# Queries and keys prepared one quad further ahead, sums of squares later, the 1e-6 added on VectorE

## The chip, the cores and the metric

The kernel runs on one core of one Trainium2 chip. The time is the device time of one launch in microseconds (us). Several runs of each kernel are made; the median is compared. One further execution is recorded by the hardware profiler, and the views shown here come from that one.

## The reference, cut to what matters

Cosine attention for 8 batches of 12 heads, 448 tokens, head size 64, followed by a two-layer network with an exact GELU over all 3584 tokens:

```
q_n = q / (norm(q) + 1e-6);  k_n = k / (norm(k) + 1e-6)
attn = softmax(q_n @ k_n.T / 0.1)            # per head, 448 x 448
x = concat of heads of (attn @ v)            # 3584 x 768
h = x @ w_in                                 # 768 -> 2048
out = gelu(h) @ w_out                        # 2048 -> 768
```

All inputs and the output are float32; the matrix products run in bf16.

## The kernel before

**Quads, units, groups.** Four heads of one batch form a *quad*; a batch has three, so there are 24, and batch b begins with quad g0 = 3b. A *unit* is what one preparation step handles: quad 0 is split in two units, and from then on unit n is quad n - 1. In `attention(b)`, `u = 3b + 1` is the unit of quad g0; in `first(b)`, `u` is the unit of the next batch's first quad. Units are put into *groups* of one or two, whose norms go through the logarithm and the exponential together.

**Preparing a quad.** `load_qk` (SyncE queue, L130) brings q and k; `square` squares both on GpSimd (L157, one instruction for 128x1792 elements); `reduce` sums each row's 64 squares on VectorE (L166). For a group, `logs` and `roots` take exp(0.5 ln(.)) on ScalarE (L173, L179 or L182), `inverses` adds 1e-6 and inverts (from group 4 on the addition is a GpSimd instruction, L191; the reciprocal is VectorE's, L193). `scale` multiplies q and k by it on GpSimd (L209, two instructions a quad) and `transposes` turns the result with a transposing DMA from the SyncE queue (L221), which gives `qkT`. Buffers: 4 for loaded quads, 2 for squares, 3 each for scaled and for turned quads.

**Attention.** `scores` (L247) makes four 64x448 products for one chunk of keys into one of three pairs of PSUM banks; `exps` (L257) takes the exponential on ScalarE. `visit(b, pairs)` does this for as many of the 21 chunks of batch b as it has pairs named, in the order of the quads; a pair can be written again when its exponential is done. `total(g)` sums the exponentials with TensorE (`sm`, L309, 16 products) and turns, adds, inverts and spreads them on VectorE (L331 to L352). `weighted(g, p)` multiplies with v (`o`, L323, 28 products) into pair p and normalises into `x` on VectorE (L357). For the first quad of a batch from the fourth batch on, the sums are taken on VectorE instead (`chunked`, L266, two instructions; `turned_all`, `inverted_all`), during `first`.

**The two layers.** `first(b)` multiplies x by w_in (`hp`, L759, 96 products) and applies GELU. The second layer (`op`, L392) is cut into single products and used as filling of the next batch's attention: `run()` issues the next 12 to 28 of them. Sixteen make one tile of 128x384, which VectorE copies out (`ot`, L396) before SyncE stores it. For every second batch the filling has 128 products (8 tiles), for the others 96 (6 tiles); I number the tiles and their copies 1 to 8 within a batch.

**Two PSUM banks are shared.** `mm_tile` gives the `op` tiles two banks in turn, and `sm` takes the bank that the next `op` tile would get:

```
t = ps_mm.tile(list(shape), dtype, tag=f"mm{turn[0] if aside is None else turn[0] ^ aside}", name=name)
if aside is None:
    turn[0] ^= 1
```

So `sm` and the next `op` tile must wait until the copy of the tile before last is done.

**Order.** `tc.manual_schedule()` keeps every engine's instructions in the order in which the program writes them. `upto(f, n)` calls step f for all units, quads or groups below n that are not done yet; where it stands decides where on every queue these instructions come.

Of the kernel before, what the change touches and what calls it, by code (L numbers as in the profile page):

```python
# [9 lines left out]
F32 = mybir.dt.float32  # L10
BF16 = mybir.dt.bfloat16
AF = mybir.ActivationFunctionType
ALU = mybir.AluOpType
# [3 lines left out]
def kernel(  # L17
# [17 lines left out]
    nc = tc.nc  # L35
    B, H, S, D = q.shape
    C = S // D
    NQ = H // 4
# [9 lines left out]
    consts = ctx.enter_context(tc.tile_pool(name="consts", bufs=1))  # L48
# [4 lines left out]
    nrm = ctx.enter_context(tc.tile_pool(name="nrm", bufs=3))  # L53
# [32 lines left out]
    nc.vector.memset(blank, 0.0)  # L86

    root2 = [consts.tile([128, 4 * C, 2], F32, name=f"root2_{n}") for n in range(2)]
    for t in root2:
        nc.vector.memset(t[:, :, 1], 1e-6)  # L90

# [21 lines left out]
    units = [(0, 0, 1), (0, 1, 2)] + [(g, 0, 2) for g in range(1, NG)]  # L113
    NU = len(units)
    groups = [[n] for n in range(NQ + 2)] + [[NQ + 2, NQ + 3], [2 * NQ + 1], [2 * NQ + 2]]
    for n in range(3 * NQ, NU, NQ):
        groups += [[n, n + 1], [n + 2]] if n + 2 < NU else [[n]]
    shapes = [[len(gr), 2, units[gr[0]][2] - units[gr[0]][1], C] for gr in groups]
    place = {u: (n, j) for n, gr in enumerate(groups) for j, u in enumerate(gr)}
    qk_t, v_t, sq_t, nq_t, rn_t, qkb_t, qkT_t, pt_t = {}, {}, {}, {}, {}, {}, {}, {}  # L120
# [47 lines left out]
    ln_t, sr_t = {}, {}  # L168
# [5 lines left out]

    def roots(n):
        ln = ln_t.pop(n)
        if n <= NQ:
            sr_t[n] = root2[n % len(root2)][:, :math.prod(shapes[n])]
            nc.scalar.activation(sr_t[n][:, :, 0], ln.rearrange("p j i s c -> p (j i s c)"), AF.Exp, scale=0.5)  # L179
        else:  # L180
            sr_t[n] = nrm.tile(list(ln.shape), F32, tag="sr", name=f"sr{n}")
            nc.scalar.activation(sr_t[n], ln, AF.Exp, scale=0.5)  # L182

    def inverses(n):
        sr = sr_t.pop(n)
        shape = [128] + shapes[n]
        se = nrm.tile(shape, F32, tag="se", name=f"se{n}")
        if n <= NQ:
            nc.vector.tensor_reduce(se.rearrange("p j i s c -> p (j i s c)"), sr, mybir.AxisListType.X, ALU.add)
        else:  # L190
            nc.gpsimd.tensor_scalar(se, sr, 1e-6, None, ALU.add)  # L191
        rn = nrm.tile(shape, F32, tag="rn", name=f"rn{n}")
        nc.vector.reciprocal(rn, se)  # L193
        rn_t[n] = rn
# [68 lines left out]
    def chunked(g, s):  # L263
        if s == 0:
            acc_t[g] = accp.tile([128, 2, S], F32, tag="acc", name=f"acc{g}")
        nc.vector.tensor_reduce(acc_t[g][:, s], all_t[g][:, :, s].rearrange("p c q -> p q c"),  # L266
                                mybir.AxisListType.X, ALU.add)

    def turned_all(g):
        tr = rcp.tile([128, 2 * NB, 32], F32, tag="tr", name=f"ta{g}")  # L270
        nc.vector.transpose(tr.rearrange("p b r -> p (b r)"), acc_t.pop(g).rearrange("p s q -> p (s q)"))
        su = bank_t[g, "su"] = rcp.tile([128, 2, 2, NB], F32, tag="sa", name=f"sa{g}")
        nc.vector.tensor_reduce(su[:, 0].rearrange("p s b -> p (s b)"), tr, mybir.AxisListType.X, ALU.add)
        for j in range(4):
            o = j ^ 1
            nc.vector.tensor_copy(su[32 * j:32 * (j + 1), 1], su[32 * o:32 * (o + 1), 0])

    def inverted_all(g):
        su = bank_t.pop((g, "su"))
# [49 lines left out]
    def turned(g):  # L329
        tr = rcp.tile([128, 2 * NB, 32], F32, tag="tr", name=f"tr{g}")[:, :NB]  # L330
        nc.vector.transpose(tr.rearrange("p b r -> p (b r)"), bank_t.pop((g, "sm"))[:, :S])  # L331
        bank_t[g, "tr"] = tr.rearrange("p b (k r) -> p k b r", k=2)
# [26 lines left out]
    def total(g):  # L359
        sums(g)  # L360
        turned(g)
        inverted(g)
        spread(g, 0)
        spread(g, 1)
# [75 lines left out]
    def upto(f, n, last=None):  # L440
        last = {load_qk: NG, load_v: NV, root: len(groups), load_wi: NQ + 1, load_wo: 4}.get(f, NU)
        while done.get(f, 0) < min(n, last):
            done[f] = done.get(f, 0) + 1
            f(done[f] - 1)
# [188 lines left out]
    def visit(b, pairs):  # L633
        for p in pairs:
            n, c = passes[at.get(b, 0)]
            at[b] = at.get(b, 0) + 1
            scores(b * NQ + n, ((0, c), (1, c)), p)
            exps(b * NQ + n, ((0, c), (1, c)))

    def attention(b, fill):  # L640
        fill = list(fill)
        if b == 1:
            parts = iter((20, 13, 14, 17, 16, 16))
        elif b == 2:
            parts = iter((20, 16, 16, 16, 16, 14, 14, 16))
        else:
            parts = iter((20, 18, 18, 18, 26, 28) if len(fill) == 128 else (14, 12, 14, 14, 20, 22))

        def run(n=None):
            for _ in range(next(parts) if n is None else n):  # L650
                fill.pop(0)()

        x_t[b] = xp.tile([128, KD, S], BF16, tag="x", name=f"x{b}")
        g0, u = b * NQ, b * NQ + 1
        run()
        upto(scale, u + 3)
        upto(transposes, u + 3)
        if b == 1:
            upto(load_qk, g0 + NQ + 2)
            upto(square, u + 4)  # L660
            visit(b, (0, 1, 2))
            run()
            visit(b, (0, 1, 2))
            run()
            upto(load_qk, g0 + NQ + 3)
            visit(b, (0, 1))
            upto(square, u + 5)
            run()
            visit(b, (0, 1, 2))
            both(g0, 0)  # L670
            upto(load_v, b + 3)
            upto(load_qk, g0 + NQ + 4)
            visit(b, (1, 2))
            upto(reduce, u + 4)
            run()
            visit(b, (1, 2, 0))
            both(g0 + 1, 1)
            visit(b, (2, 0))
            logs(6)
            roots(6)  # L680
            run()
            both(g0 + 2, 2)
            inverses(6)
            done[root] = 7
            return
        upto(scale, u + 4)
        upto(transposes, u + 4)
        if b == 2:
            visit(b, (0, 1, 2))
            run()  # L690
            upto(load_qk, g0 + NQ + 3)
            upto(square, u + 5)
            visit(b, (0, 1, 2))
            run()
            total(g0)
            visit(b, (1, 2))
            weighted(g0, 0)
            upto(load_v, b + 3)
            visit(b, (1, 2))
        else:  # L700
            visit(b, (1, 2))
            weighted(g0, 0)
            visit(b, (1, 2))
            run()
            upto(load_qk, g0 + NQ + 3)
            upto(square, u + 5)
            visit(b, (0, 1, 2))
            upto(load_v, b + 3)
        run()
        visit(b, (0, 1, 2))  # L710
        upto(reduce, u + 5)
        run()
        upto(load_qk, g0 + NQ + 4)
        total(g0 + 1)
        visit(b, (1, 2))
        weighted(g0 + 1, 0)
        visit(b, (1, 2))
        n = 2 * b + 5
        if b == 2:
            run()  # L720
            visit(b, (0,))
            total(g0 + 2)
            visit(b + 1, (1, 2))
        else:
            run()
            if b + 1 < B:
                visit(b + 1, (1, 2, 0))
            total(g0 + 2)
            if b + 1 < B:
                visit(b + 1, (1,))  # L730
        if n < len(groups):
            logs(n)
            roots(n)
            inverses(n)
            done[root] = n + 1
        if b == 2:
            run()
            visit(b + 1, (0, 1, 2))
        run()
        if b + 1 < B:  # L740
            visit(b + 1, (1, 2))
        weighted(g0 + 2, 0)
        if b + 1 < B:
            visit(b + 1, range(1, 1 + C - at[b + 1]))
        assert not fill, len(fill)

    def first(b):
# [4 lines left out]
        u = (b + 1) * NQ + 1  # L752
# [19 lines left out]
        if b == 0:  # L772
            upto(square, u + 3)
            upto(scale, u + 1)
            upto(transposes, u + 1)
            upto(load_wo, 4)
            upto(reduce, u + 3)
        else:
            late = int(b == 1)
            upto(scale, u + 2 - late)  # L780
            upto(transposes, u + 2 - late)
            upto(load_qk, (b + 1) * NQ + 5)
            upto(square, u + 4 - late)
            if 1 < b < B - 1:
                chunked((b + 1) * NQ, 0)
                chunked((b + 1) * NQ, 1)
            upto(reduce, u + 4 - 2 * late)
            if 1 < b < B - 1:
                turned_all((b + 1) * NQ)
                inverted_all((b + 1) * NQ)  # L790
# [34 lines left out]
    late = nrm.tile([128, 1], F32, tag="late", name="late", bufs=1)  # L825
# [56 lines left out]
```

## Time and profile before

| | |
|---|---|
| median of 3 runs | 422.19 us (421.31 to 422.74) |
| profiled execution, its own time | 422.47 us |
| its span from the first to the last instruction | 420.7 us |
| granted TensorE clock, mean | 1.0 |
| busy: TensorE, VectorE, ScalarE, GpSimd | 405.1, 253.0, 248.5, 167.5 us |
| instructions: TensorE, VectorE, ScalarE, GpSimd | 3423, 409, 362, 115 |
| from one batch's first `hp` to the next, batches 2 to 6 | 54.4, 48.4, 50.6, 48.4, 50.6 us |

1.8 us of the profiled time lie outside the span. The last row is read from the timeline of TensorE; the first `hp` of batches 1 to 6 are at 79.59, 133.95, 182.39, 233.00, 281.44 and 332.04 us, and the last batch's is at 376.73 us. The odd batches 3, 5 and 7 have the short filling. A line of the timeline reads: start, duration, engine, line of the program, operation, tiles, shapes, how many instructions are merged, and in brackets how long the engine was idle before and what ended that. The ends of TensorE's products are modelled, so the starts are what is read.

### The profile page before, as it was taken

Reading aid. Unit: us, or ns where it says so; the run is one execution under the profiler, and the core shown is the slowest. Engines: PE = TensorE matmul, PEld = TensorE weight load, DVE = VectorE, ACT = ScalarE, POOL = GpSimd, SP = SyncE. Lnnn points to the kernel's source line nnn. Section 1 sums busy time; section 2 is a strip of 40 time slices with the busy share of each in tenths; the row PEclk is TensorE's granted clock in tenths of the full one; section 3 lists DMA queues with packets and bytes.
Section 4 is the critical chain, followed back from the end, with each engine's and each line's share of the span. In section 5 each row is a group of like instructions: output and inputs, shape, how many; then the busy total and the mean of one; then the engine's idle time right before and its main releaser. Section 6 shows DMA issues by size and latency. Waiting matters only on the chain.

```text
span 420.7 us, 8110 instructions
## 1 busy us (share of the span) xinstructions
PE 405.1 (96%) x3423; PEld 212.0 (50%) x3423; DVE 253.0 (60%) x409; ACT 248.5 (59%) x362; POOL 167.5 (40%) x115
## 2 busy tenths in 40 slices
PE   8999999999999997999999998899999999999995
PEld 3445445555445553555555554455555555455563
DVE  5786117922666993689556894669845795360021
ACT  6995786388667575655674657575665557714300
POOL 5999615193907228080641707244180603000000
PEclk9999999999999999999999999999999999999999
DMA  8999999552693306950197802954069400330032
GB/s 291 260 256 211 202 232 305 122 132 45 122 272 108 110 1 139 263 150 24 30 187 226 170 0 47 244 158 127 2 126 221 89 0 2 83 77 1 6 77 70
DMA packets 66484, 54.53 MB, mean 130 GB/s; under 512 B 38672, under 2 KB 62352, under 8 KB 66448
## 3 DMA queue, kind: packets, MB, share of 16 engines
q1 hardware_dynamic: 54464, 41.79, 37.8%
q0 software_dynamic: 11600, 11.80, 17.4%
q8 instruction: 27, 0.44, 0.4%
q10 hardware_dynamic: 384, 0.43, 0.3%
q14 instruction: 9, 0.07, 0.1%
HBM read 45.61 MB, written 11.01 MB: 135 GB/s over the span
## 4 chain that ended last, share of the span: by engine, by line
PE 52%; issue 18%; POOL 16%; DMA 6%; ACT 5%; DVE 1%; SPq 1%; POOLq 0%; ACTq 0%; DVEq 0%
PE hp L759 22%; PE op L392 20%; POOL qkb L209 8%; POOL sq L157 6%; PE st L247 4%; DMA qkT<-qkb 4%; ACT pt L257 4%; PE o L323 2%; PE sm L309 2%; DMA qk<-in_k_dram 2%; PE op L411 1%; SPq L130 1%; ACT L815 1%; POOL v L142 1%; POOL se L191 1%
## 5 line engine op out<-in xcount | busy, mean ns | idle before, releaser
L257 ACT ACTIVATE pt<-st 128x896 bf16<-128x896 f32 x168 | 142.7, 916 | 63.6 <-PE st L247 63.2
L392 PE MATMUL op<-wo,g 128*128 128x384 bf16 x864 | 148.2, 327 | 0.0
L759 PE MATMUL hp<-x,wi 128*128 128x448 bf16 x768 | 147.1, 353 | 0.0
L392 PEld LDWEIGHTS <-g 128*128 128x128 bf16 x864 | 81.3, 98 | 62.0 <-issue 10.8
L759 PEld LDWEIGHTS <-wi 128*128 128x128 bf16 x768 | 74.4, 98 | 71.7 <-issue 3.3
L802 ACT ACTIVATE g<-hp 128x448 bf16<-128x448 f32 x128 | 65.3, 546 | 75.4 <-PE hp L759 75.1
L209 POOL TENSOR_TENSOR qkb<-qk,rn 128x896 bf16<-128x896 f32 (+1 forms) x50 | 80.2, 1630 | 15.0 <-DVE rn L193 15.0
L396 DVE COPY ot<-op 128x384 f32<-128x384 f32 x54 | 29.2, 544 | 81.6 <-PE op L392 79.5
L157 POOL TENSOR_TENSOR sq<-qk 128x1792 f32<-128x1792 f32 (+1 forms) x22 | 66.5, 3037 | 13.0 <-DMA qk<-in_k_dram 13.0
L191 POOL TENSOR_SCALAR se<-sr 128x28 f32<-128x28 f32 (+1 forms) x15 | 4.5, 302 | 156.8 <-ACT sr L182 156.8
L166 DVE TENSOR_REDUCE nq<-sq 128x28 f32<-128x1792 f32 (+2 forms) x30 | 48.4, 1636 | 22.7 <-POOL sq L157 18.9
L247 PE MATMUL st<-qkT 64*64 64x448 bf16 x672 | 51.9, 360 | 4.9 <-DMA qkT<-qkb 3.2
L266 DVE TENSOR_REDUCE acc<-pt 128x448 f32<-128x3136 bf16 x10 | 55.3, 5572 | 0.0
L323 PE MATMUL o<-pt,v 64*64 64x448 bf16 x672 | 36.8, 350 | 0.0
L357 DVE TENSOR_TENSOR x<-o,rs 128x448 bf16<-128x448 f32 x48 | 27.5, 609 | 12.0 <-PE o L323 11.7
L247 PEld LDWEIGHTS <-qkT 64*64 64x64 bf16 x672 | 17.8, 105 | 32.7 <-issue 21.7
L352 DVE STREAM_TRANSPOSE rs<-rc 128x448 f32<-128x448 f32 x48 | 28.1, 623 | 0.8
L323 PEld LDWEIGHTS <-v 64*64 64x64 bf16 x672 | 19.3, 107 | 12.7 <-issue 1.7
L331 DVE STREAM_TRANSPOSE tr<-sm 128x448 f32<-128x448 f32 x19 | 12.3, 648 | 22.1 <-PE sm L309 19.8
L309 PE MATMUL sm<-pt,ones 128*32 128x448 bf16 (+1 forms) x256 | 13.9, 332 | 3.7 <-DVE ot L396 3.5
L193 DVE RECIPROCAL rn<-se 128x28 f32<-128x28 f32 (+2 forms) x19 | 6.9, 364 | 14.3 <-POOL se L191 13.7
L343 DVE TENSOR_REDUCE tr<-tr 32x28 f32<-32x28 f32 x64 | 12.6, 196 | 1.2
(48 smaller groups left out, 144.0 us busy)
## 6 DMA issues: line engine op xcount, KB each, us to landing
qk<-in_q_dram SPq DMA_DIRECT2D x23, 448.0 KB, 6.4
qk<-in_k_dram SPq DMA_DIRECT2D x23, 448.0 KB, 7.9
out_dram<-ot SPq DMA_DIRECT2D x48, 192.0 KB, 3.4
v<-in_v_dram POOLq DMA_DIRECT2D x7, 672.0 KB, 12.1
wo<-in_moe_w_out_dram POOLq DMA_DIRECT2D x4, 768.0 KB, 13.4
wi<-in_moe_w_in_dram POOLq DMA_DIRECT2D x4, 512.0 KB, 13.8
out_dram<-ot SPq DMA_DIRECT2D x12, 96.0 KB, 2.1
wi<-in_moe_w_in_dram POOLq DMA_DIRECT2D x4, 256.0 KB, 14.1
```

The lines of the kernel that those rows point to most:

```text
L157: eng.tensor_tensor(sq[:, part], t[:, part], t[:, part], ALU.mult)
L166: nc.vector.tensor_reduce(nq[:, part], sq[:, part], mybir.AxisListType.X, ALU.add)
L209: eng.tensor_tensor(qkb[:, i, :, s0:s1].rearrange("p c s d -> p s c d"), t[:, i, s0:s1], rn[:, i].to_broadcast([128, s1 - s0, C, D]), ALU. ...
L247: nc.tensor.matmul(st[cols, n, :S], lhsT=qkT[rows, 1, c, cols], rhs=qkT[rows, 0, :, cols], start=True, stop=True, tile_position=(64 * s, 6 ...
L257: nc.scalar.activation(pt, st[:, :, :S], AF.Exp, scale=inv_tau)
L266: nc.vector.tensor_reduce(acc_t[g][:, s], all_t[g][:, :, s].rearrange("p c q -> p q c"), mybir.AxisListType.X, ALU.add)
L323: nc.tensor.matmul(bank_t[g, h][cols, :S], lhsT=v_t[g][rows, s, c, :], rhs=pt_t[g, s, c][rows], start=(c == 0), stop=(c == C - 1), tile_po ...
L352: nc.vector.transpose(rs, bank_t[g, "rc"][:, h].to_broadcast([128, NB, 32]))
L392: nc.tensor.matmul(ps[:, :NH], lhsT=g_t[sb][:, kf, t * 128:(t + 1) * 128], rhs=wo[:, kf, ni * NH:(ni + 1) * NH], start=(kf == 0), stop=(kf ...
L396: nc.vector.tensor_copy(ot[:, ni * NH:(ni + 1) * NH], ps[:, :NH])
L759: nc.tensor.matmul(hps[m], lhsT=wi[:, kd, m * 128:(m + 1) * 128], rhs=x_t[b][:, kd, :], start=(kd == 0), stop=(kd == KD - 1))
L802: nc.scalar.activation(g_t[sb][:, m, hf * S:(hf + 1) * S], hps.pop(m), AF.Gelu)
```

## The change

- `groups` are cut differently from unit 11 on: the pairs are the second and third quad of a batch, the single one is the first quad of the next batch. Before, the single one was the second quad, the pair the third and the next batch's first.
- In `first(b)`, b from 2 on, two quads are scaled and turned, where one was; at the head of the next `attention` one is left of two. Loads go one quad further ahead.
- The squares go one unit further ahead: `attention(b)` still holds one and `first(b)` two, but unit u + 4's now stands in `first(b - 1)` and unit u + 5's in `attention(b)`, after the load of v (batch 2 holds both). Of the reductions, `attention(b)` now holds two and `first(b)` one: unit u + 4's stands ahead of the third `run()` (the fourth in batch 2), unit u + 5's after `weighted(g0 + 1, 0)` and a `visit`, just ahead of the fifth `run()` (the sixth in batch 2). In `first` the one reduction stands between the two `chunked`.
- `visit(b, (1, 2))` stands ahead of `total(g0 + 1)`, where it stood behind it (in batch 2 also at `total(g0)`).
- From group 4 on the 1e-6 is added by a VectorE reduction over pairs (value, 1e-6), as it was for the earlier groups: the GpSimd instruction is gone. The four copies in `turned_all` become reductions over one element.

```diff
@@ root2
+    root2 += [consts.tile([128, 8 * C, 2], F32, name=f"root4_{n}") for n in range(1)]
@@ groups
-    for n in range(3 * NQ, NU, NQ):
-        groups += [[n, n + 1], [n + 2]] if n + 2 < NU else [[n]]
+    groups += [[3 * NQ, 3 * NQ + 1]]
+    for n in range(3 * NQ + 2, NU, NQ):
+        groups += [[n, n + 1], [n + 2]] if n + 2 < NU else [[n, n + 1]]
@@ roots(n)
-        if n <= NQ:
-            sr_t[n] = root2[n % len(root2)][:, :math.prod(shapes[n])]
-            nc.scalar.activation(sr_t[n][:, :, 0], ln.rearrange("p j i s c -> p (j i s c)"), AF.Exp, scale=0.5)
-        else:
-            sr_t[n] = nrm.tile(list(ln.shape), F32, tag="sr", name=f"sr{n}")
-            nc.scalar.activation(sr_t[n], ln, AF.Exp, scale=0.5)
+        sr_t[n] = root2[2 if len(groups[n]) == 2 else n % 2][:, :math.prod(shapes[n])]
+        nc.scalar.activation(sr_t[n][:, :, 0], ln.rearrange("p j i s c -> p (j i s c)"), AF.Exp, scale=0.5)
@@ inverses(n)
-        if n <= NQ:
-            nc.vector.tensor_reduce(se.rearrange("p j i s c -> p (j i s c)"), sr, mybir.AxisListType.X, ALU.add)
-        else:
-            nc.gpsimd.tensor_scalar(se, sr, 1e-6, None, ALU.add)
+        nc.vector.tensor_reduce(se.rearrange("p j i s c -> p (j i s c)"), sr, mybir.AxisListType.X, ALU.add)
@@ turned_all(g)
-            nc.vector.tensor_copy(su[32 * j:32 * (j + 1), 1], su[32 * o:32 * (o + 1), 0])
+            nc.vector.tensor_reduce(su[32 * j:32 * (j + 1), 1].rearrange("p s b -> p (s b)"),
+                                    su[32 * o:32 * (o + 1), 0].rearrange("p s (b n) -> p (s b) n", n=1),
+                                    mybir.AxisListType.X, ALU.add)
@@ attention(b)
         if b == 2:
             visit(b, (0, 1, 2))
             run()
-            upto(load_qk, g0 + NQ + 3)
+            upto(load_qk, g0 + NQ + 4)
             upto(square, u + 5)
             visit(b, (0, 1, 2))
             run()
+            visit(b, (1, 2))
             total(g0)
-            visit(b, (1, 2))
             weighted(g0, 0)
             upto(load_v, b + 3)
             visit(b, (1, 2))
@@
             run()
-            upto(load_qk, g0 + NQ + 3)
-            upto(square, u + 5)
+            upto(load_qk, g0 + NQ + 4)
             visit(b, (0, 1, 2))
             upto(load_v, b + 3)
+        upto(square, u + 6)
+        upto(reduce, u + 5)
         run()
         visit(b, (0, 1, 2))
-        upto(reduce, u + 5)
         run()
-        upto(load_qk, g0 + NQ + 4)
+        upto(load_qk, g0 + NQ + 5)
+        visit(b, (1, 2))
         total(g0 + 1)
-        visit(b, (1, 2))
         weighted(g0 + 1, 0)
         visit(b, (1, 2))
+        upto(reduce, u + 6)
@@ first(b)
             late = int(b == 1)
-            upto(scale, u + 2 - late)
-            upto(transposes, u + 2 - late)
+            if b == 1:
+                upto(scale, u + 1)
+                upto(transposes, u + 1)
+            for n in range(2, 4) if b > 1 else ():
+                upto(scale, u + n)
+                upto(transposes, u + n)
+                upto(load_qk, (b + 1) * NQ + 6)
             upto(load_qk, (b + 1) * NQ + 5)
-            upto(square, u + 4 - late)
+            upto(square, u + 3 if b == 1 else u + 5)
             if 1 < b < B - 1:
                 chunked((b + 1) * NQ, 0)
+                upto(reduce, u + 4)
                 chunked((b + 1) * NQ, 1)
```

## The prediction

> **What bounds the kernel now.** I read the page first: TensorE is busy 405.1 of 420.7 us, the others 60% or less, so the end moves only with TensorE's stops. The waits, asked for TensorE alone, name them (total, times, longest):
>
> ```profile
> PE sm L309 <- DVE ot L396: 3.5, 2, 1.8
> PE st L247 <- DMA qkT<-qkb: 3.2, 4, 1.1
> ```
>
> The timeline of TensorE places them. In batch 3:
>
> ```profile
> 159.77 2.45 PE L392 MATMUL op<-wo,g 128*128 128x384 bf16 x14
> 163.35 0.76 PE L247 MATMUL st<-qkT 64*64 64x448 bf16 x12 [1.13 <-DMA qkT<-qkb]
> 164.04 2.45 PE L392 MATMUL op<-wo,g 128*128 128x384 bf16 x14
> 168.25 0.85 PE L309 MATMUL sm<-pt,ones 128*32 128x448 bf16 x16 [1.76 <-DVE ot L396]
> 169.03 0.57 PE L247 MATMUL st<-qkT 64*64 64x448 bf16 x8
> 169.43 1.50 PE L323 MATMUL o<-pt,v 64*64 64x448 bf16 x28
> 170.75 0.87 PE L247 MATMUL st<-qkT 64*64 64x448 bf16 x8
> 171.56 3.42 PE L392 MATMUL op<-wo,g 128*128 128x384 bf16 x20
> ```
>
> Starts, not ends, give the prices. Unstopped, 14 `op` take 2.37 to 2.38, 16 `sm` 0.78, 28 `o` 1.33, 12 `st` 0.69, 8 `st` 0.46 (0.40 where `o` follows). So the first stop costs 163.35 - 159.77 - 2.37 = 1.21, the second 168.25 - 164.04 - 2.37 = 1.84, and the 8 `st` at 170.75 take 0.81, 0.35 too long: their pair waits for the exponential of the `st` at 169.03. Batch 5 repeats all three, batch 7 the first (0.86) and third; 4, 6 and, twice, 2 have the third only. VectorE shows who made the second:
>
> ```profile
> 165.71 2.02 DVE L166 TENSOR_REDUCE nq<-sq 128x28 f32<-128x1792 f32 x1 [4.20 <-POOL sq L157]
> 167.65 0.55 DVE L396 COPY ot<-op 128x384 f32<-128x384 f32 x1
> ```
>
> A reduction stood at the head of VectorE's queue waiting for GpSimd's square; the copy behind it frees the bank that `sm` wants. This is the pattern to carry into the changed order.
>
> **The change, batch by batch.** All starts below are the rows of before, moved by what has gone or come earlier.
>
> *Batches 3 and 5, gains.* The second quad is turned during `first`, so qkT is there: -1.21. The reduction ahead of the third `run` has a square finished in `first`: -1.84. `st` ahead of `sm` puts 0.40 + 0.78 + 1.33 between it and the next `st`, against 0.44 to ScalarE's start and two exponentials of 0.87: -0.35. Together -3.40.
>
> *Batches 3 and 5, what is late next.* The second reduction now stands between the normalisation of g0 + 1 and copy 4. In before, `turned` to the end of `weighted` takes VectorE 169.15 to 173.43, 4.28. From the batch's first `op` TensorE needs 2.37 + 0.40 + 1.33 + 0.80 + 2.05 + 0.69 + 2.37 + 0.69 + 2.37 + 0.40 = 13.5 up to `sm` (the first long `st`, at 0.80, stays). `turned` follows 0.90 behind, so `weighted` ends at 13.5 + 0.90 + 4.28 = 18.7; the reduction takes 1.95, to 20.6; copy 4 0.55, to 21.2. `sm` of g0 + 2 wants that bank at 20.0 (13.5 + 0.78 + 1.33 + 0.46, then 20 `op` 3.3 and 12 `st` 0.69): 1.2 of stop. Net -2.2 each.
>
> *Batches 4 and 6.* Gain 0.35. Copy 5 stands behind the same reduction. `sm` comes 3.34 + 0.40 + 1.33 + 0.80 + 3.03 + 0.69 + 3.03 + 0.69 + 3.03 + 0.40 = 16.74 after the first `op`: normalisation ends at 16.74 + 0.90 + 4.28 = 21.9, the reduction at 23.9, copy 5 at 24.45. Tile 7 wants its bank after 16.74 + 0.78 + 1.33 + 0.46 = 19.31 and 22 `op` more, at 22.9. Stop 1.6, net +1.2 each. In before copy 5 ended 1.1 ahead of tile 7, so 1.95 does not fit in.
>
> *Batch 7.* No reduction is left: -0.86 - 0.35 = -1.2.
>
> *Batch 2.* Gain 0.35 twice. But here the second reduction is quad 11's, whose square waits for a load issued in this very batch; the square and the load were followed by an idle stretch before. Rows (SyncE's timeline, the issues with their us to landing, TensorE's timeline):
>
> ```profile
> 114.73 0.61 SPq L130 DMA_DIRECT2D qk<-in_k_dram  x1
> qk<-in_k_dram SPq DMA_DIRECT2D x1, 448.0 KB, 8.4
> 121.76 2.45 PE L392 MATMUL op<-wo,g 128*128 128x384 bf16 x14
> 124.14 0.38 PE L247 MATMUL st<-qkT 64*64 64x448 bf16 x4
> 124.54 0.84 PE L309 MATMUL sm<-pt,ones 128*32 128x448 bf16 x14
> 125.84 0.57 PE L247 MATMUL st<-qkT 64*64 64x448 bf16 x8
> ```
>
> k of quad 11 lands at 114.73 + 8.4 = 123.1; SyncE's queue ahead of it (two turning DMAs, one store) is unchanged. Square 3.17, to 126.3; reduction 2.0, to 128.3; copy 6 0.6, to 128.9; only then `sm`. TensorE is at that `sm` at 123.6 (124.14 + 0.19 for 4 `st`, less 0.7): 5.3 us of standstill. The next `st` start at 128.9 + 0.78 = 129.7 instead of 125.84: +3.85. The reduction ahead of the fourth `run` has its square at 113.8 and ends at 116.6; copy 4 at 117.1 is just in time for tile 6 at 117.3.
>
> *Sum without the clock:* +3.85 - 2 x 2.2 + 2 x 1.2 - 1.2 = about +0.6.
>
> *The clock.* No stop of before reaches 2 us, so no row prices one of 5.3. Two rows are near. The clock record holds 1.00 after the last product (415.9) and then drops:
>
> ```profile
> 418.00:420.00 2.00, 0.00 (x0) 0.00 (x0) 0.00 (x0) 0.00 (x0) 0.00 (x0) 1.00 0.02 2
> 420.00:420.70 0.70, 0.00 (x0) 0.00 (x0) 0.00 (x0) 0.00 (x0) 0.00 (x0) 0.71 0.00 0
> ```
>
> (seventh column the granted clock). A mean of 0.71 over 0.70 us is a fall to one half at about 420.3, 4.4 after the last product, sooner than the 5.3 here. And at the start 17 of the first `spin` products take 1.93 to 7.0, 5.07, where a 448-column product takes 0.19 later: 1.9 lost until full speed. So bounds are 0 and 1.9; I take 1.9, the row of a clock coming back, since 5.3 exceeds 4.4.
>
> [...]
>
> *At nothing:* the 1e-6. GpSimd loses 15 instructions (4.5 us busy) that ended long before the next use; VectorE gains about 14 of 0.22 (row L189) to 0.35, beside 168 us idle, and at a batch's end they stand after the spreads and ahead of copies that nobody wants for 1 us or more. The reductions that replace copies in `turned_all` (0.21 against 0.19 each) stand in `first`, where VectorE has one reduction of 1.95 fewer; should GpSimd's squares hold it, the chain ends at `first`'s end + 2.8 against + 3.2 before. GpSimd does four scalings and two squares in `first`, 13 us of the 18.2. Buffers released for the earlier loads and turns were free a batch ahead. Without this cover each us late in `first` would cost one only when `x` is wanted, 4.7 into the next batch.
>
> **Sum and forecast.** +0.6 + 1.9 = +2.5 on the profiled execution's 422.47 (span 420.7 plus 1.8). That execution lies 0.28 above the median of 422.19; I put the difference on the median: 424.6.
>
> **Rivals.**
> - *The clock holds through the gap.* [...] Then +0.6: 422.8, no change.
> - *Faster: quad 11 lands early.* One place, batch 2. Other loads of k land sooner: the one issued at 61.30 took 5.4. With 5.4 it lands at 120.1, the standstill shrinks by 3.0 to 2.3, the clock stays, and the sum is +0.6 - 3.0 = -2.4: 419.8. It decides from a landing 0.6 ahead of my 123.1, and shows over the noise from 1.9 ahead, 121.2. For it: the queue behind changes. Against: the profile's DMA engines are about full from 112 to 127.
> - *Slower still.* The next load (quad 12) now follows directly, ahead of a store, and shares the engines; landing at 10.1, the slowest k row of that stretch, adds 1.7: 426.3.
>
> **How the numbers follow.** A measurement of this kernel can tell about 0.3%, 1.3 us, from no change. Forecast 0.47, clock holds 0.32, early landing 0.15, late landing 0.06. Slower: 0.9 x 0.47 + 0.25 x 0.32 + 0.06 = 0.56. Faster: 0.75 x 0.15 + 0.1 x 0.32 = 0.15. Same: the remaining 0.29. Range 420.3 to 426.6: from half of the early landing to the forecast with its clock cost doubled, the late landing within it; the forecast's own case is 423.3 to 426.6.
>
> **What would show it.** Right: no wait for qkT in batches 3, 5, 7; in batch 2 one wait of TensorE for `ot` of 5 us, its VectorE row a reduction released by GpSimd's square, and that by k's DMA; waits of 1.2 to 1.6 before `sm` or `op` in batches 3 to 6; a granted clock under 1.00 after 129. `hp` to `hp`: batch 2 58 to 60, 3 and 5 46.2, 4 and 6 51.8. Wrong: batch 2 within 1 us of 54.4, or batches 4 and 6 at 50.3, which would mean that copies are not held behind the reductions.

## The result and the profile after

| | before | changed |
|---|---|---|
| median, 13 runs each | 421.66 us (420.79 to 427.72) | 423.64 us (422.37 to 424.87) |
| profiled execution, its span | 422.47, 420.7 us | 423.36, 421.6 us |
| first `hp` to first `hp`, batches 2 to 7 | 54.36, 48.44, 50.61, 48.44, 50.60, 44.69 us | 59.73, 46.27, 51.93, 46.26, 51.92, 43.64 us |
| granted TensorE clock, mean | 1.0 | 0.992 |

The ratio of the medians is 1.0047, 95% interval 1.0032 to 1.0063: the changed kernel is slower, by 2.0 us. The six differences of the third row are +5.37, -2.17, +1.32, -2.18, +1.32 and -1.05, together +2.61. The changed program numbers its lines a little differently: `st` is L242, `sm` L306, `op` L389, `ot` L393, the square L159 and the reduction L168.

The waits of TensorE alone in the changed kernel that bear on this (total, times, longest):

```profile
PE sm L306 <- DVE ot L393: 5.9, 3, 3.9
PE op L389 <- DVE ot L393: 2.7, 2, 1.4
PE st L242 <- DMA qkT<-qkb: 0.4, 1, 0.4
PE st L242 <- DVE x L354: 0.3, 1, 0.3
```

The four waits for `qkT` have become one of 0.4, in batch 1; none is left in batches 3, 5 and 7. Waits for copies (`ot`) have grown from 3.5 to 5.9 + 2.7, and one of them alone is 3.9. TensorE's timeline finds it in batch 2:

```profile
120.64 2.45 PE L389 MATMUL op<-wo,g 128*128 128x384 bf16 x14
123.36 0.38 PE L242 MATMUL st<-qkT 64*64 64x448 bf16 x4 [0.27 <-DVE x L354]
127.64 1.50 PE L306 MATMUL sm<-pt,ones 128*32 128x448 bf16 x16 [3.90 <-DVE ot L393]
129.07 0.96 PE L242 MATMUL st<-qkT 64*64 64x448 bf16 x8
129.97 3.67 PE L389 MATMUL op<-wo,g 128*128 128x384 bf16 x14
133.57 0.76 PE L242 MATMUL st<-qkT 64*64 64x448 bf16 x12
```

TensorE comes to `sm` at 123.36 + 0.19 = 123.55 and starts it at 127.64: 4.1 of standstill. What follows is also slow: from start to start `sm` takes 1.43 instead of 0.78, 14 `op` 3.60 instead of 2.37. The timelines of GpSimd and VectorE show the chain that TensorE stood behind:

```profile
121.91 3.16 POOL L159 TENSOR_TENSOR sq<-qk 128x1792 f32<-128x1792 f32 x1 [8.05 <-DMA qk<-in_k_dram]
125.10 2.02 DVE L168 TENSOR_REDUCE nq<-sq 128x28 f32<-128x1792 f32 x1 [1.80 <-POOL sq L159]
127.04 0.55 DVE L393 COPY ot<-op 128x384 f32<-128x384 f32 x1
```

Quad 11's keys release the square, the square the reduction, and only behind the reduction comes the copy that frees `sm`'s bank. The clock record (seventh column) accounts for the slow products:

```profile
122.00:124.00 2.00, 1.47 (x11) 0.65 (x10) 1.30 (x3) 0.51 (x2) 2.00 (x1) 1.00 1.11 330
124.00:126.00 2.00, 0.00 (x0) 0.00 (x0) 0.90 (x1) 0.71 (x1) 1.07 (x1) 0.91 1.04 403
126.00:128.00 2.00, 0.36 (x7) 0.17 (x10) 1.59 (x2) 0.00 (x0) 0.00 (x0) 0.50 0.67 258
128.00:130.00 2.00, 2.00 (x25) 0.56 (x18) 0.78 (x2) 0.23 (x1) 0.00 (x0) 0.50 0.66 159
130.00:132.00 2.00, 2.00 (x11) 0.99 (x8) 1.86 (x8) 1.97 (x4) 0.00 (x0) 0.50 0.19 49
132.00:134.00 2.00, 2.00 (x21) 0.92 (x19) 1.48 (x4) 0.01 (x1) 0.73 (x1) 0.88 0.00 0
```

A mean of 0.91 over 2 us is 1.64 at full and 0.36 at half: it fell at 125.64. The 0.88 puts the return at 132.48. The clock was at one half for 6.84 us, from 2.1 us after the last product on. That is this execution, with a mean clock of 0.992; 5 of the 13 have 0.996, by an estimate half as long at half speed (0.004 x 421.6 x 2 = 3.4 us).

Batches 3 (first) and 4 (second), VectorE and then TensorE:

```profile
175.75 2.00 DVE L168 TENSOR_REDUCE nq<-sq 128x28 f32<-128x1792 f32 x1
177.67 0.55 DVE L393 COPY ot<-op 128x384 f32<-128x384 f32 x1
...
225.27 2.00 DVE L168 TENSOR_REDUCE nq<-sq 128x28 f32<-128x1792 f32 x1
227.19 1.01 DVE L393 COPY ot<-op 128x384 f32<-128x384 f32 x2
```

```profile
176.52 0.76 PE L242 MATMUL st<-qkT 64*64 64x448 bf16 x12
178.27 0.85 PE L306 MATMUL sm<-pt,ones 128*32 128x448 bf16 x16 [0.99 <-DVE ot L393]
...
222.69 3.75 PE L389 MATMUL op<-wo,g 128*128 128x384 bf16 x22
227.79 0.81 PE L389 MATMUL op<-wo,g 128*128 128x384 bf16 x4 [1.36 <-DVE ot L393]
```

Here the reductions wait for nothing; they run between the normalisation and a copy, and TensorE stops 178.27 - 176.52 - 0.69 = 1.06 and 227.79 - 222.69 - 3.58 = 1.52 (3.58 is 22 `op` in a longer run of them, 0.163 each).

### The profile page after: what moved, and what is told of

Same layout as the page of the kernel before. It is cut to its first block, busy times and chain, and to the rows that moved or that the text cites. A ratio compares the mean times of both kernels' runs of the same rounds, so it can differ in the third digit from the quotient of the medians.

```text
span 421.6 us, 8092 instructions
## 1 busy us (share of the span) xinstructions
PE 405.8 (96%) x3423; PEld 210.8 (50%) x3423; DVE 256.5 (61%) x423; ACT 248.4 (59%) x360; POOL 163.0 (39%) x100
## 4 chain that ended last, share of the span: by engine, by line
PE 79%; DVE 8%; DMA 5%; POOL 3%; ACT 3%; issue 1%; SPq 0%; POOLq 0%
PE hp L757 30%; PE op L389 28%; PE st L242 8%; PE o L320 4%; DVE nq L168 3%; PE sm L306 3%; DMA qkT<-qkb 3%; ACT pt L252 2%; DMA qk<-in_k_dram 2%; PE spin L446 2%; POOL sq L159 1%; POOL qkb L204 1%; PE op L408 1%; PE sm L297 1%; DVE tr L340 1%
## 5 line engine op out<-in xcount | busy, mean ns | idle before, releaser
L389 PE MATMUL op<-wo,g 128*128 128x384 bf16 x864 | 149.7, 328 | 2.7 <-DVE ot L393 2.7
L389 PEld LDWEIGHTS <-g 128*128 128x128 bf16 x864 | 81.7, 98 | 67.3 <-issue 16.8
L393 DVE COPY ot<-op 128x384 f32<-128x384 f32 x54 | 29.0, 545 | 81.8 <-PE op L389 79.8
L159 POOL TENSOR_TENSOR sq<-qk 128x1792 f32<-128x1792 f32 (+1 forms) x22 | 66.6, 3042 | 21.9 <-DMA qk<-in_k_dram 21.8
L168 DVE TENSOR_REDUCE nq<-sq 128x28 f32<-128x1792 f32 (+2 forms) x30 | 48.7, 1634 | 15.0 <-POOL sq L159 12.1
L242 PE MATMUL st<-qkT 64*64 64x448 bf16 x672 | 50.8, 361 | 1.5 <-DMA qkT<-qkb 0.4
L242 PEld LDWEIGHTS <-qkT 64*64 64x64 bf16 x672 | 17.1, 105 | 27.6 <-issue 19.7
L306 PE MATMUL sm<-pt,ones 128*32 128x448 bf16 (+1 forms) x256 | 14.2, 344 | 5.9 <-DVE ot L393 5.9
L306 PEld LDWEIGHTS <-ones 128*32 128x32 bf16 x256 | 5.7, 97 | 12.7 <-issue 11.5
L186 DVE TENSOR_REDUCE se<-root 128x28 f32<-128x56 f32 (+2 forms) x18 | 3.8, 213 | 12.1 <-ACT root L180 12.0
```

The lines of the kernel that those rows point to most:

```text
L159: eng.tensor_tensor(sq[:, part], t[:, part], t[:, part], ALU.mult)
L168: nc.vector.tensor_reduce(nq[:, part], sq[:, part], mybir.AxisListType.X, ALU.add)
L242: nc.tensor.matmul(st[cols, n, :S], lhsT=qkT[rows, 1, c, cols], rhs=qkT[rows, 0, :, cols], start=True, stop=True, tile_position=(64 * s, 6 ...
L306: nc.tensor.matmul(bank_t[g, "sm"][r:r + 32, cols], lhsT=ones, rhs=pt_t[g, s, c][:, cols], start=(c < 2), stop=(c >= C - 2), tile_position ...
L389: nc.tensor.matmul(ps[:, :NH], lhsT=g_t[sb][:, kf, t * 128:(t + 1) * 128], rhs=wo[:, kf, ni * NH:(ni + 1) * NH], start=(kf == 0), stop=(kf ...
L393: nc.vector.tensor_copy(ot[:, ni * NH:(ni + 1) * NH], ps[:, :NH])
```

## The experiments

My theory: all that the change loses comes from one thing, the second reduction standing ahead of copies; in batch 2 the load of quad 11 makes it long, and the clock falls on top. Rivals: the load and the clock are the loss, and the place of the reduction is not; or the loss in the later batches comes from the new order of `st` and `sm`, or of the scalings. All variants but `st_first` are made from the changed kernel.

### The second reduction behind the copies, in every batch and in batch 2 alone

`late_all` moves one line behind the `run()` whose copies it held up; `late_b2` does so in batch 2 alone.

```diff
         visit(b, (1, 2))
-        upto(reduce, u + 6)
         n = 2 * b + 5
         if b == 2:
             run()
+            upto(reduce, u + 6)
 ...
         else:
             run()
+            upto(reduce, u + 6)
```

> The changed kernel with the second reduction (unit u + 5's) moved behind the fifth run() (the sixth in batch 2), so that the copies of that run stand ahead of it on VectorE; the instructions are the same. Theory (VectorE's fixed order: the reduction holds the copies, and in batch 2 it waits for a load): all the new stops go, 1.0 each in batches 3 and 5, 1.5 in 4 and 6, and in batch 2 the 4.0 with the 2.3 that the fallen clock costs: hp to hp 53.4 in batch 2, 45.2 in 3 and 5, 50.4 in 4 and 6; 411 to 413 us, ratio to the kernel before 0.977, clock 1.00 throughout. Rival (the transfers that now follow each other, or the reduction's 2 us itself, are what TensorE waits for, wherever it stands): the stops come back at the next sm or op, 422 to 424 us.

> The same move in batch 2 alone. Theory: the part of batch 2 goes and the stops in batches 3 to 6 stay: 6.3 less than the changed kernel, 417 to 418 us, ratio to the kernel before 0.990; hp to hp 53.4 in batch 2, the others as in the changed kernel (46.3, 51.9, 46.3, 51.9). Rival: as above, no gain; or, if batch 2's delay is what disturbs the later batches, those get shorter too and the time is that of the move in all batches.

`late_all`: 412.83, ratio 0.9802 (0.9787 to 0.9817). `late_b2`: 418.0, 0.9928 (0.9913 to 0.9943). Batches 2 to 7 of `late_all` take 54.11, 45.21, 50.41, 45.21, 50.41, 43.64, those of `late_b2` 54.11, 46.27, 51.92, 46.26, 51.92, 43.63. So batch 2 gives back 5.62 and the four others 1.06, 1.52, 1.05 and 1.51, just the stops read above: 10.8 together, as from 423.64 to 412.83. In batch 2 about 6.3 was expected (53.4 for the 54.11 that came). The missing 0.7 was hidden behind the standstill: the 4 `st` take 0.46 up to `sm`, where 0.19 was counted (0.40 in the kernel before), and `sm` 1.24 for 0.78 (1.30 in the kernel before, where TensorE's bracket names an exponential). VectorE and TensorE of `late_all` in batch 2:

```profile
123.37 0.54 DVE L393 COPY ot<-op 128x384 f32<-128x384 f32 x1
125.65 2.02 DVE L168 TENSOR_REDUCE nq<-sq 128x28 f32<-128x1792 f32 x1 [1.75 <-POOL sq L159]
127.59 0.64 DVE L328 STREAM_TRANSPOSE tr<-sm 128x448 f32<-128x448 f32 x1
```

```profile
123.50 0.38 PE L242 MATMUL st<-qkT 64*64 64x448 bf16 x4 [0.26 <-DVE x L354]
123.96 1.31 PE L306 MATMUL sm<-pt,ones 128*32 128x448 bf16 x16
125.20 0.57 PE L242 MATMUL st<-qkT 64*64 64x448 bf16 x8
```

Quad 11's keys come no sooner and the reduction still waits 1.75, but the copy is now ahead of it and `sm` starts at once. The theory holds, and this version beats both kernels: by 2.0% the one before, and by 2.4% the changed one (0.9802 / 1.0047).

### The standstill filled with idle products

To price the clock alone, `spin_gap` puts 20 products that no one reads into the gap of batch 2.

```diff
             run()
             visit(b, (0,))
+            gap = pair(1, "gap")
+            for _ in range(20):
+                nc.tensor.matmul(gap[:, 0, :S], lhsT=ident, rhs=blank, start=True, stop=True)
             total(g0 + 2)
```

> The changed kernel with 20 idle products (128x448, some 0.19 us each, 3.7 us together, results unused, into a free pair of banks) put on TensorE ahead of batch 2's last sums, where it stands still for 4.0 us: the wait stays and only the clock is kept busy. Theory (the standstill takes the clock down, and that costs by itself): the granted clock stays 1.00, sm, st and op behind the gap run at 0.78, 0.5 and 2.4 us instead of 1.43, 0.9 and 3.6: 2.3 us less than the changed kernel, 421.3 us, ratio to the kernel before 0.999; hp to hp 57.4 in batch 2. Rival (the clock's record changes but the slow products hide a wait for exponentials or copies): no gain, 423.6.

421.96, ratio 1.0017 (1.0001 to 1.0033); the granted clock is 1.0 and batch 2 takes 58.09. TensorE's timeline:

```profile
123.91 3.96 PE L722 MATMUL gap<-blank,ident 128*128 128x448 bf16 x20
128.50 0.85 PE L306 MATMUL sm<-pt,ones 128*32 128x448 bf16 x16 [0.64 <-DVE ot L393]
129.28 0.57 PE L242 MATMUL st<-qkT 64*64 64x448 bf16 x8
129.79 2.45 PE L389 MATMUL op<-wo,g 128*128 128x384 bf16 x14
```

`sm` is at its usual 0.78 and 14 `op` at 2.37. From `sm` to the next batch's first `hp` it is 8.89, in the changed kernel 11.15: the clock cost 2.26 in that execution (2.77 in the profile of `changed_again`, 11.66 there). The rest of the loss stays, since the copy is as late as before (0.62 later, counted from batch 1's first `hp`, because the keys landed later in this execution; hence 1.64 less in batch 2 and not 2.26).

### The load of quad 11 earlier

```diff
+                    upto(load_qk, 12)
                     upto(square, u + 4)
```

The line stands in `first(1)`, so that the keys land sooner and the order on VectorE stays.

> The changed kernel with quad 11's load issued some 18 us earlier, in the first layer of batch 1, once its buffer is free; nothing else is moved. Theory (in batch 2 the load is late, and the reduction hands its lateness to the copy and to TensorE): the square is done long before, so the reduction runs as soon as the normalisation ends (some 122.9 to 124.9 on the changed kernel's scale), copy 6 by 125.5, and sums start there instead of at 127.6. A stop of 1.9 is left, of the kind seen in batches 3 to 6, and if that is short enough for the clock, the 2.3 go too: hp to hp 55.3 in batch 2, 419.3 us, ratio to the kernel before 0.996 (with the clock fallen 421.6, 1.001). Rival (the place of the reduction alone is what counts): 59.7 and 423.6 as in the changed kernel.

421.01, ratio 0.9984 (0.9965 to 1.0003); batch 2 takes 55.57 in the profiled execution, where the reduction starts at 123.33 and no longer waits for the square. VectorE, then TensorE:

```profile
125.25 0.54 DVE L393 COPY ot<-op 128x384 f32<-128x384 f32 x1
```

```profile
125.85 0.85 PE L306 MATMUL sm<-pt,ones 128*32 128x448 bf16 x16 [2.00 <-DVE ot L393]
```

A stop of 125.85 - 123.46 - 0.19 = 2.2 is left, made by the reduction's own length (the bracket, which goes by modelled ends, has 2.00). The twelve executions split in two: six with a mean clock of 1.0 (419.2 to 421.14, median 419.4) and six with 0.996 (420.96 to 422.33, median 421.1). All six of `late_b2`, which lacks this stop, have 0.998 or more. So one stop of 2.2 in a stream of products seems to cost 1.7 more in half of the executions; the profiled one is among the six where the clock held, so no trace shows the fall itself. This is the prediction's rival of an early landing, made to happen: 419.8 forecast, 419.4 where the clock stays up.

### The order of scores and sums

`st_first` is the kernel before with only `visit(b, (1, 2))` ahead of `total`, in batch 2 at g0 (shown) and in batches 2 to 7 at g0 + 1; `ahead_only` is `late_all` with `visit` behind `total` again.

```diff
-            total(g0)
             visit(b, (1, 2))
+            total(g0)
```

> The kernel before with one part of the change alone: the visit of pairs 1 and 2 ahead of total(g0 + 1), and in batch 2 also of total(g0). Theory: a wait of 0.35 for exponentials goes at seven places; in batches 3 and 5 the scores (0.4) moreover fill part of the stop ahead of the sums: 5 x 0.35 + 2 x 0.75 = 3.2 less than before, 418.5 us, ratio 0.992. Rival (TensorE's products are merely put in another order, and sums 0.4 later make everything behind them 0.4 later): no difference, 421.7.

> The late reduction in all batches, with the scores behind the sums again as in the kernel before: what is left of the change is the preparation one quad ahead, with its waits mended. Theory: the stops for qkT and for copies stay away (no wait of TensorE for either), and the wait for exponentials, measured at 0.2 a place, comes back at seven places, less the 0.27 that the scores of pair 0 in batch 2 now wait: 412.8 + 7 x 0.2 - 0.27 = 414.0 us, ratio to the kernel before 0.983. Rival (the order of scores and sums is what removes the stops): TensorE waits for copies again, 417 us or more.

`st_first`: 419.0, ratio 0.9942 (0.993 to 0.9954), batches 2 to 7 at 54.18, 47.74, 50.41, 47.73, 50.41, 44.50. `ahead_only`: 414.59, 0.9842 (0.9816 to 0.9869), at 54.29, 45.41, 50.60, 45.41, 50.61, 43.83. The order is worth 0.18 to 0.20 a batch, where the prediction took 0.35. In 3 and 5 `st_first` gains 0.70, because the scores also fill part of the stop before `sm`, as its waits of TensorE show (1.3 at most, for 1.8 before):

```profile
PE sm L309 <- DVE ot L396: 2.5, 2, 1.3
```

The larger gain in 3 and 5, from 48.44 to the 45.41 of `ahead_only`, is that of the units further ahead and the moved reductions.

### Why the order gave 0.20 and not 0.35

The rows of `late_all` show where the rest went. In batch 3:

```profile
164.58 0.57 PE L242 MATMUL st<-qkT 64*64 64x448 bf16 x8
165.08 0.85 PE L306 MATMUL sm<-pt,ones 128*32 128x448 bf16 x16
165.86 1.52 PE L320 MATMUL o<-pt,v 64*64 64x448 bf16 x28
167.21 0.55 PE L242 MATMUL st<-qkT 64*64 64x448 bf16 x8
167.69 3.42 PE L389 MATMUL op<-wo,g 128*128 128x384 bf16 x20
```

The four steps take 167.69 - 164.58 = 3.11, in the kernel before 171.56 - 168.25 = 3.31. The last 8 `st` wait no more: 0.48 for 0.81. But the 8 that were moved take 0.50 ahead of `sm`, where they took 0.40 ahead of `o`, and `o` takes 1.35 for 1.32. That makes 0.33 - 0.10 - 0.03 = 0.20. The prediction had 0.46 for 8 `st` ahead of `op`, which no row shows (0.48 to 0.51 unstopped), and left the moved ones at 0.40.

Another long stretch of `st` is at the head of batches 3 to 7. `late_fill` is `late_all` with two `op` moved between `weighted(g0, 0)` and the next `visit` in batches 3 to 7, which gives ScalarE 0.33 more.

```diff
-            parts = iter((20, 18, 18, 18, 26, 28) if len(fill) == 128 else (14, 12, 14, 14, 20, 22))
+            parts = iter((20, 16, 18, 18, 26, 28) if len(fill) == 128 else (14, 10, 14, 14, 20, 22))
 ...
             weighted(g0, 0)
+            run(2)
             visit(b, (1, 2))
```

> The late reduction in all batches, and two products of the second layer taken from the second run() and put between weighted(g0, 0) and the visit behind it, in batches 3 to 7, where 8 st take 0.80 for 0.48. Theory (those st wait for the exponential of the visit before): the two products of 0.33 fill the wait, 5 x 0.32 = 1.6 less: 411.2 us, ratio to the kernel before 0.9765. Rival (ScalarE's exponentials bound that stretch): no gain, 412.8.

412.71 for the expected 411.2, ratio 0.9797 (0.9773 to 0.9821), at 54.10, 45.13, 50.32, 45.12, 50.32, 43.55. The gain over `late_all` is 0.08 or 0.09 a batch. TensorE in batch 3 of `late_fill`:

```profile
155.42 1.49 PE L320 MATMUL o<-pt,v 64*64 64x448 bf16 x28
156.84 0.50 PE L389 MATMUL op<-wo,g 128*128 128x384 bf16 x2
157.27 0.57 PE L242 MATMUL st<-qkT 64*64 64x448 bf16 x8
157.78 1.80 PE L389 MATMUL op<-wo,g 128*128 128x384 bf16 x10
```

From start to start the 8 `st` take 0.51, for 0.80 in `late_all`, so a wait there is gone. But `o` takes 1.42 for 1.33 and two `op` 0.43 for 0.34 (14 take 2.37): by an estimate from these starts each passage between 64x64 tiles and the full array costs about 0.1, and two more passages take back most of the gain. Other rows fit: 16 `op` take 2.71 and 28 take 4.65, so 0.163 each and 0.1 once, and 8 `st` take 0.40 ahead of `o`, on tiles of the same size, but 0.48 to 0.51 ahead of `op` or `sm`. That the passages are the reason is inferred from these starts; no run measured one by itself.

### The 1e-6 on GpSimd again

`gp_add` undoes that one edit in the changed kernel, `late_gp` in `late_all`. `gp_add_again` and `changed_again` repeat the pair on one chip.

```diff
-        sr_t[n] = root2[2 if len(groups[n]) == 2 else n % 2][:, :math.prod(shapes[n])]
-        nc.scalar.activation(sr_t[n][:, :, 0], ln.rearrange("p j i s c -> p (j i s c)"), AF.Exp, scale=0.5)
+        if n <= NQ:
 ...
+        else:
+            sr_t[n] = nrm.tile(list(ln.shape), F32, tag="sr", name=f"sr{n}")
+            nc.scalar.activation(sr_t[n], ln, AF.Exp, scale=0.5)
 ...
+            nc.gpsimd.tensor_scalar(se, sr, 1e-6, None, ALU.add)
```

> The changed kernel with the 1e-6 added on GpSimd again, from group 4 on, as before. Theory: both places lie beside other work, no difference from the changed kernel: 423 to 424 us, ratio to the kernel before 1.005. Rival (the way over GpSimd delays the scaling, or VectorE's added instructions delay the copies): over 1 us off that, in either direction.

> The changed kernel as it is, once more, as the base of the two beside it: 423.6 by both theories (422.4 to 424.9 before), ratio 1.005; batch 2 59.5 to 60.0 from its first hp to batch 3's.

> The changed kernel with the 1e-6 added on GpSimd again, once more and beside the changed kernel. Theory: GpSimd's addition (0.35) and its handing on delay the scaling and so the load of quad 11's keys, and TensorE waits for that load: 0.5 to 1.2 above the kernel beside it, all in batch 2 (60.3 to 60.8). Rival: the load's landing scatters between chips and executions and the addition costs nothing: within 0.4 of the kernel beside it, 423.6.

> Every reduction behind the batch's last copy (the version with the sums of squares late in all batches, 412.8), and the 1e-6 on GpSimd again. Theory: nobody on TensorE waits for quad 11's load there, so the addition is hidden: 412.8, ratio 0.980, periods as without it. Rival: the addition costs its time wherever it stands, in every batch: 414 to 415, ratio 0.984 to 0.986.

`gp_add`: 425.19, ratio 1.0093 (1.0068 to 1.0118). `changed_again`: 424.29, 1.0064 (1.0029 to 1.0098). `gp_add_again`: 424.49, 1.0079 (1.005 to 1.0109). `late_gp`: 413.4, 0.98 (0.9761 to 0.984). SyncE's queue in the changed kernel, and in `gp_add`:

```profile
111.49 1.19 SPq L378 DMA_DIRECT2D out_dram<-ot  x2
...
113.38 0.57 SPq L132 DMA_DIRECT2D qk<-in_k_dram  x1
```

```profile
112.17 1.71 SPq L385 DMA_DIRECT2D out_dram<-ot  x2
...
114.57 0.62 SPq L132 DMA_DIRECT2D qk<-in_k_dram  x1
```

From batch 1's first `hp` (79.06 and 79.43) the keys' load is issued at 34.32 and at 35.14. `changed_again` and `gp_add_again` have 34.30 and 35.11, before has 35.14: GpSimd's addition delays the load by 0.82 and 0.81. Of that 0.26 is its own (the scaling starts at 24.47 for 24.21); the rest comes at the two stores ahead of the load, whose issue takes 1.71 for 1.19, and why is open. What it costs is not settled: 1.55 in the first pair (measured in separate sessions), against the "no difference" expected, and 0.20 in the second, where 0.5 to 1.2 was expected and the rival had "within 0.4". The time from issue to the square scatters as much (8.53, 9.05, 8.60 and 8.14 in the order changed, `changed_again`, `gp_add`, `gp_add_again`), so that batch 2 of the profiles takes 59.73, 60.75, 60.54 and 60.01. That it costs something is likely: in the second pair 5 of the 12 executions of `changed_again` lie under 423.85, the lowest of the 11 of `gp_add_again`. Where nobody on TensorE waits for that load, the edit costs nothing that shows: 0.9800 against 0.9802.

## Why the prediction was right, and where it was not

*The sign and the size.* Forecast 424.6, measured 423.64 and, again, 424.29. The mechanism is as told: in batch 2 a reduction that waits for a square, that for keys, with a copy behind it; `late_b2` and `late_all` show it by removing it. Some of the terms came out only because errors in them cancel.

*Batch 2's standstill.* Forecast +3.85 without the clock. The 8 `st` behind `sm` start 50.01 after batch 1's first `hp`, before 46.25: +3.76, of which the slow `sm` is 0.65. So the term is +3.11, 0.7 too large. The step that failed is "SyncE's queue ahead of it (two turning DMAs, one store) is unchanged": it held two stores by the trace, and the load went out 0.82 sooner, for the addition taken from GpSimd, which the prediction had put "at nothing" (undone in `gp_add`, the load is back at 35.14). The copy was so done 48.58 after that `hp`, not 49.31. The standstill shrank by more, from 5.3 to 4.1, because TensorE came 0.48 later than thought: 14 `op` to the 4 `st` took 2.72 for 2.38 (the bracket names 0.27 for the normalisation), and the earlier order of `st` had brought less.

*The clock.* Forecast 1.9, measured 2.26 (with `spin_gap`). The 1.9 was misread: by the profile 14 `spin` products, not 17, take 1.93 to 7.0, so that row loses 5.07 - 14 x 0.19 = 2.4; and the clock record has 1.00 from 0 to 11 there, so that the clock made them slow was not shown. And the argument, that 5.3 exceeds the 4.4 seen after the last product, was no good: the standstill was 4.1, below that row, and by it the clock should have held. It fell 2.1 us after the last product here, 2.8 in the profile of `gp_add` (a granted clock of 0.69 from 126 to 128), and 3.7 in `changed_again`, whose clock record has:

```profile
126.00:128.00 2.00, 0.00 (x0) 0.00 (x0) 0.64 (x1) 0.46 (x1) 1.32 (x1) 1.00 1.04 402
128.00:130.00 2.00, 0.10 (x4) 0.10 (x7) 1.84 (x2) 0.00 (x0) 0.00 (x0) 0.74 0.36 138
```

(0.74 puts the fall at 128.96; the last product ended at 125.30.) All 41 executions of the changed kernel and of `gp_add`, their repeats included, show a mean clock of 0.996 or less, so the chance given to a clock that holds, 0.32, was too high. Two faults cancelled, a standstill taken too long and a threshold taken too high: that this term came out is luck.

Once down, it stayed at half for the same time in both profiles of the changed kernel, 6.84: from 125.64 to 132.48, and from 128.96 to 135.80 in `changed_again`. The length of a standstill alone does not tell in these rows whether it falls. The stop of 1.84 in the kernel before and the one of 2.2 in the profile of `early_load` left the record at 1.00, but 6 of the 12 executions of `early_load` have a mean of 0.996; the changed kernel lost the clock 2.1 into a standstill, and the kernel before kept it for 4.4 after its last product. What else decides was not shown.

*Batches 3 and 5.* Forecast -2.2, measured -2.17 and -2.18. The waits for `qkT` and for the square's copy went as told. The stop was 1.06 for 1.2, and `st` ahead of `sm` brought 0.20 for 0.35; that the two cancel is luck as well. Without the stop, `late_all` has 48.44 - 45.21 = 3.23 for the 3.40 of the sum.

*Batches 4 and 6.* Forecast +1.2, measured +1.32: the stop 1.52 (for 1.6) less 0.20 (for 0.35).

*Batch 7.* -1.05 for -1.2, the same 0.15.

*The sum and its base.* +2.61 for +2.5. The profiled execution as a whole is only 0.9 longer: batch 1's first `hp` is at 79.06 for 79.59 (it is at 80.81 in `changed_again`), and the time from the last batch's first `hp` to the end is about 1.2 shorter, because the last store landed after 2.1 instead of 3.3. These are scatter (from the last batch's first `hp` to the end it is 42.7 in `late_all`, `changed_again` and `st_first`, for 44.0 in the kernel before); later runs of before have medians of 421.1 to 421.7, below the 422.19 of three runs that the sum was put on. That sum, 422.19 + 2.5, is 424.7 and not 424.6; and half of the early landing's -2.4 would put the low end of the range at 421.0, not 420.3.

*Rivals.* The early landing was the right quantity at a smaller size: 0.8 sooner, seen from the same `hp`. That is more than the 0.6 from which it was to decide, and the clock fell all the same; to show it needed 1.9. The late landing did not come: with quad 12's load directly behind, quad 11's keys still took 8.4 to landing, as before.

## What to carry to other kernels

A step on an in-order queue is not priced by its own length but by what stands behind it: put a reduction that waits for a load behind the copies that free banks, not ahead of them, even if its engine is idle 40% of the time (VectorE was busy for 253.0 of 420.7 us). Moving that single line turned 0.5% slower into 2% faster. When a step is dropped from one engine, follow the chain it stood in to the next load before calling it free.

## What the runs showed of the hardware that was not expected

- TensorE's clock fell 2.1 us into one standstill and 3.7 into another, and with a single stop of 2.2 the mean clock was lowered, to 0.996, in 6 of 12 executions (`early_load`). Once down it stayed at half for 6.84 us in both profiles of the changed kernel, 4.8 and 5.9 us of it with TensorE busy; the losses were 2.26 and 2.77.
- From start to start, products on 64x64 tiles take longer where tiles of another shape follow: `o` 1.42 ahead of `op` and 1.33 ahead of `st` (`late_fill` and `late_all`), 8 `st` 0.48 to 0.51 ahead of `op` or `sm` and 0.40 ahead of `o`. About 0.1 us a passage is an estimate from these starts; in a sum it reads like a wait, but the timeline names none there.
- The issue of two stores on SyncE in batch 2 took 1.71 us in the profiles of the kernel before, `gp_add`, `gp_add_again` and `late_gp`, which add 1e-6 on GpSimd in a 0.35 us instruction some 9 us earlier, and 1.19 in those of the changed kernel, `changed_again` and `late_all`, which do not. The cause is open.
